# Moving the splits of Wo and the turns of the attention output in the last units of a fused transformer block

## The chip, the cores and the metric

The kernel runs on one core of a Trainium2 chip. The metric is the time of one execution on the device, in microseconds (us). It was run three times; the median is 1302.93 us (1302.89 to 1303.72). The profile comes from one further execution of 1301.86 us.

The engines are named as the profile names them: TensorE (PE; PEld is its weight load), VectorE (DVE), ScalarE (ACT), GpSimd (POOL), and SyncE (SP), which only issues DMA transfers here. Each engine works through its own list of instructions in the order in which the program lists them.

## The reference

For one sequence of S = 2048 tokens with D = 576 values each, the block adds three things: the input, an attention over eight dilated neighbours, and a mixer with an MLP of F = 4608 hidden values.

```python
xn = _layernorm(x)
# attention: 32 heads of 18; token s looks at s, s-2, ..., s-14
qkv = xn @ wqkv
logits = einsum("bhsd,bhswd->bhsw", q, kg) * scale
o = einsum("bhsw,bhswd->bhsd", softmax(logits), vg)
A = o @ wo
# mixer: shift four channel groups by +1, -1, +2, -2 tokens
h = gelu(_layernorm(xn) @ w1)
x1 = xn + shifted(h) @ w2
B = x1 + gelu(_layernorm(x1) @ w3) @ w4
return x + A + B
```

All matmuls work on pairs of a rounded part ("hi") and the rest ("lo") of each operand, and add up the products hi·hi, hi·lo and lo·hi, so that the result has the precision of 32-bit floats.

## The kernel before

The program is one function, `fused_block`. The order of instructions on each engine is the order in which the Python code emits them: nothing is rescheduled. First come the projections to q, k and v, then the mixer, then a long loop that holds the MLP, and at last the output phase.

**The loop over units** (line 759). The MLP is cut into 18 chunks c of 256 hidden values and 4 blocks b of 512 tokens, so 72 units (c, b). A unit has an *up* part and a *down* part:

- `up(c, b, i)`, for i = 0 and 1: 14 matmuls of 128x512 into one accumulator (line 676). ScalarE then makes the gelu twice: hi (line 680) and g32 (line 681, called g in the profile). VectorE makes lo = g32 - hi (line 682).
- `down(*prev, j)`, for j = 0 to 3: the second matmul of the *previous* unit, for token tile j of 128 tokens, 12 matmuls of 128x288 (line 696) into an accumulator `ps`. VectorE then adds it to Y (line 699; "the addition" below). The accumulators come from the pool `psb`, a ring of three: a fourth tile can be begun only when the first of the three has been added.

In the units before the last six, VectorE works on the attention in between, in small steps. The last six units have extra work, written by hand into the loop. They are numbered from the end: z = u - 72, so z = -6 to z = -1. After z = -1 come four more down tiles (line 828), for the unit z = -1 itself, and then the output phase (line 835).

**What is prepared there.** The output phase multiplies the attention output by Wo, tile by tile of 128 tokens (t = 0 to 15), with the transposed attention output standing. Two things have to be ready for it:

- *Wo as hi and lo.* `load_wo(k)` loads a part of Wo into the buffer `rawf` (two buffers): k = 0 and k = 2 are two slices of 128 rows each, k = 4 is the remaining 64 rows, loaded twice. `split_wo(k)` (by way of `split_w`) rounds it on ScalarE (line 167) and subtracts on VectorE (line 168). The three calls are the first, second and last part of Wo.
- *The attention output, transposed, as hi and lo,* in four blocks b of 512 tokens. `load_o(b)` loads a block in token order. `o_turn(b, t)` turns one of its four tiles on VectorE with two transposes of 32x32 squares (lines 129 and 130) into the staging tile ST (`st` in the profile, of which there is one). After the fourth tile, `put` writes ST to DRAM in four transfers (line 137; `xd`), and `get` reads the block back transposed in two (line 142) into a tile that `o_block` provides: `xt` for blocks 0 and 1, the tiles `x1n` of the MLP's input for blocks 2 and 3. `split_x` makes hi and lo of it (lines 148 to 155), half by half.

Before the change these calls stood as follows.

| unit | before the up part | in the up part | between the down tiles | after |
|---|---|---|---|---|
| z = -5 | | | `o_turn(0, j)` | `load_o(2)` |
| z = -4 | `load_wo(0)` | `get` of block 0 | `o_turn(1, j)` | `load_o(3)` |
| z = -3 | `split_wo(0)`, `load_wo(2)` | `get` of block 1 | `split_x` of block 0 | |
| z = -2 | `split_wo(2)`, `load_wo(4)` | `o_turn(2, 0)` to `o_turn(2, 3)` | | `get` of block 2 |
| z = -1 | `split_wo(4)` | `split_x` of block 1 | `o_turn(3, j)` | |
| last four tiles | | | `get` of block 3 behind j = 0; `split_x` of block 2 | |

`split_x` of block 3 stands in the output phase, at t = 4 and 5.

Of the kernel before, what the change touches and what calls it, by code (L numbers as in the profile page):

```python
# [45 lines left out]
def fused_block(ctx, tc, x, wqkv, wo, w1, w2, w3, w4, out):  # L46
# [80 lines left out]
    def turn(src, t):  # L127
        c = slice(32 * t, 32 * t + 32)
        dve.transpose(ST[:, 4:20, c], src[:, :512].rearrange("p (j c) -> p j c", c=32))  # L129
        dve.transpose(ST[:, 0:4, c].rearrange("p (a j) c -> p a j c", a=2),  # L130
                      src[:, 512:].rearrange("p (j c) -> p j c", c=32)[:, None, :, :]
                      .to_broadcast([128, 2, 2, 32]))

    def put(key):
        xd[key] = dram.tile([5, 128, 512], F32, name="xd", bufs=4)
        for q in range(4):
            sp.dma_start(dram_ap(xd[key], 128 * q, [[512, 32], [32 * 512, 20], [1, 128]]),  # L137
                         ST[32 * q:32 * q + 32])

    def get(key, xt):  # L140
        for k in ((0, 3), (3, 5)):
            sp.dma_start(xt[:, 4 + k[0]:4 + k[1], :].bitcast(F32),
                         xd[key][k[0]:k[1]].rearrange("k p c -> p k c"))

    def split_x(xt, part=None):
        raw = xt.bitcast(F32)
        if part != 1:
            act.copy(RT[64:128, :], raw[64:128, 4, :])
            act.copy(xt[0:64, 4, :], raw[0:64, 4, :])
            dve.tensor_tensor(xt[64:128, 4, :], raw[64:128, 4, :], RT[64:128, :].bitcast(F32),  # L150
                              op=ALU.subtract)
        for h in range(2) if part is None else (part,):
            hi, lo = slice(2 * h, 2 * h + 2), slice(2 * h + 5, 2 * h + 7)
            act.copy(xt[:, hi, :], raw[:, lo, :])
            dve.tensor_tensor(xt[:, lo, :], raw[:, lo, :], raw[:, hi, :], op=ALU.subtract)
# [10 lines left out]
    def split_w(dst_hi, dst_lo, raw):  # L166
        act.copy(dst_hi, raw)  # L167
        dve.tensor_tensor(dst_lo, raw, dst_hi.bitcast(F32), op=ALU.subtract)  # L168
# [44 lines left out]
    def ring_block(key):  # L213
        if key not in xring:
            xring[key] = ring.tile([128, 9, 512], F32R, name="xt", tag="xt")
        return xring[key]
# [290 lines left out]
    def split_w3(f):  # L507
        if f >= NF:
            return
        t = W3[f] = wp.tile([128, 10, 128], F32R, name="W3", bufs=3)  # L510
        split_w(t[:, 0:5, :], t[:, 5:10, :], raws[f][:, :640].rearrange("p (k c) -> p k c", k=5))
# [9 lines left out]
    def n_turn(t, zpool):  # L521
        z = zpool.tile([128, D], F32, name="rz", tag="rz")
        act.activation(z, Y[:, t, :], AF.Identity, bias=RS[2][:, t, 0:1], scale=RS[2][:, t, 1:2])
        turn(z, t % 4)
        if t % 4 == 3:
            put(("n", t // 4))
# [130 lines left out]
    def bg(us, late=True):  # L657
        if state["gen"] is None or state["done"]:
            return
        state["debt"] = min(state["debt"] + us, 1.5)  # L660
        while state["debt"] > 0 and (late or not state["hold"]):
            cost = next(state["gen"], False)
            if cost is False:
                state["done"] = True
                return
            state["hold"] = cost is None
            state["debt"] -= cost or 0.0
# [4 lines left out]
    def up(c, b, i):  # L672
        f = c * C + i
        ps = psa.tile([128, 512], F32, name="p1", tag="a")
        for n, (a, w) in enumerate(PAIRS):
            pe.matmul(ps, W3[f][:, w, :], x1n[b][:, a, :], start=n == 0, stop=n == len(PAIRS) - 1)  # L676
        hi = hp.tile([128, 512], F32R, name=f"hi{i}")
        g32 = hp.tile([128, 512], F32, name="g32")
        lo = hp.tile([128, 512], F32R, name=f"lo{i}")
        act.activation(by_token(hi), in_order(ps), AF.Gelu_apprx_tanh)  # L680
        act.activation(by_token(g32), in_order(ps), AF.Gelu_apprx_tanh)  # L681
        dve.tensor_tensor(lo, g32, hi.bitcast(F32), op=ALU.subtract)  # L682
        hid[c, b, i] = (hi, lo)
# [26 lines left out]
    def open_wo():  # L710
        nonlocal wop, opool, Wo
        apc.__exit__(None, None, None)
        wop = tc.tile_pool(name="wop", bufs=1, reuse_waits="tile")
        opool = wop.__enter__()
        Wo = opool.tile([128, 10, D], F32R, name="Wo")
# [3 lines left out]
    def load_wo(k):  # L719
        r = worw[k] = wp.tile([128, 640 + D], F32, name="rawf", bufs=2)  # L720
        if k < 4:
            sp.dma_start(r[:, :2 * D].rearrange("p (k c) -> p k c", k=2),
                         wo[k * 128:(k + 2) * 128, :].rearrange("(k p) c -> p k c", p=128))
        else:
            dup_tail(r[:, :D], wo, 0, D)

    def split_wo(k):
        n = 2 if k < 4 else 1
        split_w(Wo[:, k:k + n, :], Wo[:, 5 + k:5 + k + n, :],
                worw[k][:, :n * D].rearrange("p (k c) -> p k c", k=n))  # L730
# [3 lines left out]
    def load_o(b):  # L734
        if b < NB:
            otile[b] = opool.tile([128, 4, D], F32, name="ot", bufs=2)
            for q in range(4):
                sp.dma_start(otile[b][32 * q:32 * q + 32], quads(od, b, q))

    def load_xa(t):  # L740
        xagain[t] = tp.tile([128, D], F32, name="rz", tag="rz")
        sp.dma_start(xagain[t], xf[t * 128:(t + 1) * 128, :])

    def o_turn(b, t):
        turn(otile[b][:, t, :], t)
        if t == 3:
            put(("o", b))

    def o_block(b):
        if b < 2:  # L750
            xo[b] = ring_block(("o", b))
        else:
            xo[b] = xp.tile([128, 9, 512], F32R, name=f"x1n{b}")
        return xo[b]
# [4 lines left out]
    for u, (c, b) in enumerate(units):  # L759
        if u == 2:  # L760
            ap_pool = apc.__enter__()
            state["gen"] = attention(ap_pool)
            next(state["gen"])
        r = RATE[b] / 6 if u >= 4 else 0.0
        z = u - NU
        if z == -6:
            while not state["done"]:
                bg(1e9)
            open_wo()
            load_o(0)  # L770
            load_o(1)
        if z == -4:
            load_wo(0)
        if z == -3:
            split_wo(0)
            load_wo(2)
        if z == -2:
            split_wo(2)
            load_wo(4)
        if z == -1:  # L780
            split_wo(4)
        for i in range(C):
            bg(r, False)
            up(c, b, i)
            if (u, i) in ((0, 0), (1, 0)):
                get(("n", u + 2), x1n[u + 2])
            for t in LATE.get((u, i), ()):
                n_turn(t, tp)
            if u in (1, 2) and i == 0:
                split_x(x1n[u + 1], 0)  # L790
            if z in (-4, -3) and i == 1:
                get(("o", z + 4), o_block(z + 4))
            if z == -2:
                o_turn(2, 2 * i)
                o_turn(2, 2 * i + 1)
            if z == -1:
                split_x(xo[1], i)
        if b == 3:
            split_w3(2 * c + 3)
        if prev is not None:  # L800
            for j in range(4):
                bg(r, j == 1)
                down(*prev, j)
                if u in (1, 2) and j == 1:
                    split_x(x1n[u + 1], 1)
                if z in (-5, -4, -1):
                    o_turn({-5: 0, -4: 1, -1: 3}[z], j)
                if z == -3 and j > 1:
                    split_x(xo[0], j - 2)
            if z in (-5, -4):  # L810
                load_o(z + 7)
            if z == -2:
                get(("o", 2), o_block(2))
        if b == 1:
            split_w3(2 * c + 2)
        if b == 2:
            split_w4(2 * c + 2)
            load_f(2 * c + 4)
        if b == 0 and c > 0:
            split_w4(2 * c + 1)  # L820
            load_f(2 * c + 3)
        if 4 <= u < 4 + 4 * NT:
            if u % 4 == 0:
                load_xa(u // 4 - 1)
            if u % 4 == 2:
                add_x(u // 4 - 1)
        prev = (c, b)
    for j in range(4):
        down(*prev, j)
        if j == 0:  # L830
            get(("o", 3), o_block(3))
        if j > 1:
            split_x(xo[2], j - 2)
# [51 lines left out]
```

## Time and profile before

| | |
|---|---|
| median of three runs | 1302.93 us (1302.89 to 1303.72) |
| profiled execution | 1301.86 us, its span 1300.1 us |
| TensorE busy | 1287.7 us, 99% |
| TensorE's weight loads | 1186.9 us, 91% |
| VectorE busy | 935.5 us, 72% |
| ScalarE busy | 361.7 us, 28% |
| GpSimd busy | 38.1 us, 3% |
| granted TensorE clock, mean | 0.997 |

The span is the time from the first to the last instruction. A line of a timeline reads: start in us from the span's start, length in us, engine, line of the program, operation, output <- inputs, shape and type, count; several like instructions in a row are one line, and square brackets give the idle time of the engine just before and what ended it. The names are those of the program with buffer numbers left out. "SPq" is the issue of a transfer by SyncE, and its length is that of the issue, not of the transfer. The granted clock is the share of TensorE's full clock that it was given in a stretch.

### The profile page before, as it was taken

What the parts mean: (1) busy time and instruction counts of PE and PEld (TensorE: products, weight loads), DVE (VectorE), ACT (ScalarE), POOL (GpSimd) and SP (SyncE); (2) the same over time, 40 slices, a digit from 0 to 9 for tenths busy, and PEclk for the clock granted to TensorE, in tenths of its full rate; (3) what the DMA queues carried; (4) which work ended last, traced back from release to release, by engine and by line L of the source; (5) the groups of instructions that cost most, each with busy time, mean ns of one, the idle gap of its engine ahead of it and who ended that gap; (6) DMA issues with size and microseconds to landing.
All of it is one profiled execution on the core that took longest, in us unless ns stands there. A gap on an engine that the chain in (4) does not pass through costs nothing.

```text
span 1300.1 us, 18507 instructions
## 1 busy us (share of the span) xinstructions
PE 1287.7 (99%) x7678; PEld 1186.9 (91%) x7678; DVE 935.5 (72%) x1336; ACT 361.7 (28%) x601; POOL 38.1 (3%) x108
## 2 busy tenths in 40 slices
PE   8999999999999999999999999999999999999898
PEld 8999998899899899999989899999999899999798
DVE  6456535778676778888878888878898877946642
ACT  3322226515422222132232232132232232122300
POOL 2011100021000000000000000000000000000000
PEclk9999999999999999999999999999999999999899
DMA  7646874345602120231221222122222102058542
GB/s 211 155 111 145 172 164 145 102 123 138 214 29 72 40 89 20 81 100 33 68 81 40 81 72 90 44 69 64 66 73 81 43 26 81 20 120 208 154 145 83
DMA packets 157828, 125.20 MB, mean 96 GB/s; under 512 B 72608, under 2 KB 129824, under 8 KB 157744
## 3 DMA queue, kind: packets, MB, share of 16 engines
q1 hardware_dynamic: 157744, 124.02, 34.4%
q8 instruction: 60, 0.98, 0.3%
q14 instruction: 24, 0.20, 0.0%
HBM read 83.56 MB, written 39.39 MB: 95 GB/s over the span
## 4 chain that ended last, share of the span: by engine, by line
PE 93%; DMA 3%; DVE 3%; SPq 1%; ACT 0%; issue 0%; POOL 0%; DVEq 0%
PE ps L696 33%; PE p L676 33%; PE ps L182 18%; PE ps L431 4%; PE ps L276 3%; DMA xd<-st 2%; DVE st L129 1%; DMA xt<-xd 1%; PE ps L446 1%; SPq L137 1%; PE ps L104 0%; DVE Y L699 0%; DMA x1n<-xd 0%; DVE bn L86 0%; PE p L853 0%
## 5 line engine op out<-in xcount | busy, mean ns | idle before, releaser
L696 PE MATMUL ps<-W,hi 128*128 128x288 f32 x2304 | 399.8, 295 | 5.2 <-DVE Y L699 5.2
L696 PEld LDWEIGHTS ps<-W,hi 128*128 128x128 f32 x2304 | 340.3, 188 | 12.1 <-DVE Y L699 5.7
L680 ACT ACTIVATE hi<-p 128x512 fp32r<-128x512 f32 x144 | 86.2, 598 | 576.1 <-PE p L676 576.1
L696 PE MATMUL ps<-W,lo 128*128 128x288 f32 x1152 | 245.8, 295 | 0.0
L676 PE MATMUL p<-x1n,W 128*128 128x512 f32 x1008 | 236.0, 391 | 0.0
L676 PE MATMUL p<-xt,W 128*128 128x512 f32 x1008 | 234.5, 389 | 0.0
L676 PEld LDWEIGHTS p<-x1n,W 128*128 128x128 f32 x1008 | 188.4, 189 | 37.2
L699 DVE TENSOR_TENSOR Y<-ps,Y 128x576 f32<-128x576 f32 x288 | 212.1, 749 | 13.5 <-PE ps L696 13.5
L676 PEld LDWEIGHTS p<-xt,W 128*128 128x128 f32 x1008 | 187.3, 188 | 36.9
L682 DVE TENSOR_TENSOR lo<-g,hi 128x512 fp32r<-128x512 f32 x144 | 99.4, 691 | 158.1 <-ACT g L681 158.0
L696 PEld LDWEIGHTS ps<-W,lo 128*128 128x128 f32 x1152 | 185.9, 188 | 0.0
L182 PE MATMUL ps<-WQ,xt 128*128 128x432 f32 x672 | 134.4, 359 | 0.0
L182 PEld LDWEIGHTS ps<-WQ,xt 128*128 128x128 f32 x672 | 125.5, 188 | 5.4
L628 DVE TENSOR_TENSOR prod<-q,k 128x1152 f32<-128x1152 f32 x64 | 86.4, 1350 | 0.0
L631 DVE TENSOR_REDUCE L<-prod 128x64 f32<-128x1152 f32 x64 | 86.2, 1347 | 0.0
L681 ACT ACTIVATE g<-p 128x512 f32<-128x512 f32 x144 | 85.3, 592 | 0.0
L612 DVE TENSOR_TENSOR o<-o,prod 128x1152 f32<-128x1152 f32 x56 | 75.6, 1350 | 0.0
L608 DVE TENSOR_TENSOR prod<-v,L 128x1152 f32<-128x1152 f32 x56 | 75.6, 1350 | 0.0
L167 ACT CAST W<-rawf 128x640 fp32r<-128x640 f32 x72 | 50.3, 700 | 70.5 <-PE ps L696 69.2
L168 DVE TENSOR_TENSOR W<-rawf,W 128x640 fp32r<-128x640 f32 x72 | 56.3, 785 | 0.0
L182 PE MATMUL ps<-W,h 128*128 128x288 f32 x384 | 53.5, 295 | 0.0
L182 PEld LDWEIGHTS ps<-W,h 128*128 128x128 f32 x384 | 51.9, 188 | 0.1
(108 smaller groups left out, 888.2 us busy)
## 6 DMA issues: line engine op xcount, KB each, us to landing
xd<-st SPq DMA_DIRECT2D x48, 320.0 KB, 6.0
qkvd<-stg SPq DMA_DIRECT2D x24, 432.0 KB, 3.5
rawf<-in_B_w_dram SPq DMA_DIRECT2D x36, 288.0 KB, 3.1
rawf<-in_B_w_dram SPq DMA_DIRECT2D x36, 256.0 KB, 2.9
xt<-xd SPq DMA_DIRECT2D x8, 768.0 KB, 5.1
xin<-in_A_x_dram SPq DMA_DIRECT2D x16, 288.0 KB, 3.8
q<-qkvd SPq DMA_DIRECT2D x8, 576.0 KB, 3.9
k<-qkvd SPq DMA_DIRECT2D x8, 576.0 KB, 5.6
```

The lines of the kernel that those rows point to most:

```text
L168: dve.tensor_tensor(dst_lo, raw, dst_hi.bitcast(F32), op=ALU.subtract)
L182: pe.matmul(ps[:, h, :n], xs(a), ws(b, h), start=i == 0, stop=i == len(PAIRS) - 1)
L608: dve.tensor_tensor(dst, vv, Lf[:, :, w:w + 1].to_broadcast([128, TPP * GH, HD]), op=ALU.mult)
L612: dve.tensor_tensor(o, o, dst, op=ALU.add)
L628: dve.tensor_tensor(prod.rearrange("p (j h) d -> p j (h d)", h=GH), q, k[:, r0:r0 + TPP, :], op=ALU.mult)
L631: dve.tensor_reduce(Lf[:, :, w], prod, axis=AX.X, op=ALU.add)
L676: pe.matmul(ps, W3[f][:, w, :], x1n[b][:, a, :], start=n == 0, stop=n == len(PAIRS) - 1)
L680: act.activation(by_token(hi), in_order(ps), AF.Gelu_apprx_tanh)
L681: act.activation(by_token(g32), in_order(ps), AF.Gelu_apprx_tanh)
L682: dve.tensor_tensor(lo, g32, hi.bitcast(F32), op=ALU.subtract)
L696: pe.matmul(ps[:, k, :HF], h[:, col], w[:, p, k * HF:(k + 1) * HF], start=n == 0, stop=n == len(seq) - 1)
L699: dve.tensor_tensor(yv, ps[:, :, :HF], yv, op=ALU.add)
```

## The change

Five calls are moved. No call is added or dropped.

- `split_wo(2)` goes from the start of z = -2 to the start of z = -1.
- `split_wo(4)` goes from the start of z = -1 to behind the first of the last four down tiles.
- The four turns of block 2 go from the up part of z = -2 (two behind each `up`) to between the down tiles of z = -2 (one behind each).
- The four turns of block 3 stay between the down tiles of z = -1, but two stand behind each of the last two tiles, not one behind each of the four.
- `get` of block 2 goes from the end of z = -2 to the second half of the up part of z = -1.

```diff
         if z == -2:
-            split_wo(2)
             load_wo(4)
         if z == -1:
-            split_wo(4)
+            split_wo(2)
...
-            if z == -2:
-                o_turn(2, 2 * i)
-                o_turn(2, 2 * i + 1)
+            if z == -1 and i == 1:
+                get(("o", 2), o_block(2))
...
-                if z in (-5, -4, -1):
-                    o_turn({-5: 0, -4: 1, -1: 3}[z], j)
+                if z in (-5, -4, -2):
+                    o_turn({-5: 0, -4: 1, -2: 2}[z], j)
+                if z == -1 and j > 1:
+                    o_turn(3, 2 * j - 4)
+                    o_turn(3, 2 * j - 3)
...
-            if z == -2:
-                get(("o", 2), o_block(2))
...
     for j in range(4):
         down(*prev, j)
         if j == 0:
+            split_wo(4)
             get(("o", 3), o_block(3))
```

In the lists of instructions below, a line is line of the program, operation, output <- inputs, and the shape of the output; numbers behind names tell buffers apart.

On VectorE, in unit z = -2 as it was: behind the last subtraction for block 0 (line 155) of z = -3 come the second part of Wo, then lo of the first `up`, then the first turns of block 2.

```order
 L168 TENSOR_TENSOR Wo<-rawf,Wo 128x1152
-L682 TENSOR_TENSOR lo_10945<-g_10944,hi_10943 128x512
-L129 STREAM_TRANSPOSE st<-ot 128x16x32
-L130 STREAM_TRANSPOSE st<-ot 128x4x32
-L129 STREAM_TRANSPOSE st<-ot 128x16x32
-L130 STREAM_TRANSPOSE st<-ot 128x4x32
-L682 TENSOR_TENSOR lo_10970<-g_10969,hi_10968 128x512
```

Two more turns follow, and only then the four additions (line 699). With the change the same place has both lo and the first addition ahead of the first turn, and each further addition ahead of a turn:

```order
 L155 TENSOR_TENSOR xt<-xt 128x1024
+L682 TENSOR_TENSOR lo_10943<-g_10942,hi_10941 128x512
+L682 TENSOR_TENSOR lo_10964<-g_10963,hi_10962 128x512
+L699 TENSOR_TENSOR Y<-ps,Y 128x576
+L129 STREAM_TRANSPOSE st<-ot 128x16x32
+L130 STREAM_TRANSPOSE st<-ot 128x4x32
+L699 TENSOR_TENSOR Y<-ps,Y 128x576
```

The subtraction for Wo's second part has moved behind the fourth turn.

On ScalarE, in the same unit: the cast of Wo's second part (128x1152) stood ahead of the four gelus, and now stands behind them.

```order
 L154 CAST xt<-xt 128x1024 x2
+L680 ACTIVATE hi_10941<-p_10926 128x512
+L681 ACTIVATE g_10942<-p_10926 128x512
+L680 ACTIVATE hi_10962<-p_10947 128x512
+L681 ACTIVATE g_10963<-p_10947 128x512
 L167 CAST Wo<-rawf 128x1152
-L680 ACTIVATE hi_10943<-p_10928 128x512
-L681 ACTIVATE g_10944<-p_10928 128x512
```

On VectorE, in unit z = -1 and the last four down tiles, with the change: behind the additions of the tiles j = 0 to 2 stand two turns of block 3, then the addition of j = 3 and two more turns; the first of the last four additions follows, and behind it the last part of Wo (128x576).

```order
+L129 STREAM_TRANSPOSE st<-ot 128x16x32
+L130 STREAM_TRANSPOSE st<-ot 128x4x32
+L699 TENSOR_TENSOR Y<-ps,Y 128x576
+L168 TENSOR_TENSOR Wo<-rawf,Wo 128x576
+L699 TENSOR_TENSOR Y<-ps,Y 128x576 x2
+L150 TENSOR_TENSOR x1n_11086<-x1n_11086,rt 64x512
+L155 TENSOR_TENSOR x1n_11086<-x1n_11086 128x1024
+L699 TENSOR_TENSOR Y<-ps,Y 128x576
```

The piece begins with the last of these turns. Before, each turn stood behind one addition, and the last part of Wo ahead of the unit.

On SyncE the order of the transfers is the same before and after, since the moved `get` still stands between the two `put` of blocks 2 and 3. On GpSimd nothing moves.

## The prediction

> **What bounds the kernel.** I read three views in this order: the chain that ended last, the list of what TensorE waited for, and the timeline of TensorE around its longest wait. The first two:
>
> ```profile
> PE 93%; DMA 3%; DVE 3%; SPq 1%; ACT 0%; issue 0%; POOL 0%; DVEq 0%
> ...
> PE ps L696 <- DVE Y L699: 5.2, 2, 4.6
> ```
>
> TensorE sets the time, so work on another engine counts only where TensorE waits for it. In the large matmul phases it waited twice, 5.2 us in all, and one wait is 4.6 of it. The timeline shows that one in unit z = -2:
>
> ```profile
> 1198.11 6.52 PE L676 MATMUL p<-x1n,W 128*128 128x512 f32 x28
> 1204.47 0.69 PE L696 MATMUL ps<-W,hi 128*128 128x288 f32 x4
> ...
> 1213.97 1.33 PE L696 MATMUL ps<-W,hi 128*128 128x288 f32 x4 [4.58 <-DVE Y L699]
> ...
> 1217.01 7.88 PE L676 MATMUL p<-x1n,W 128*128 128x512 f32 x28
> 1224.73 0.69 PE L696 MATMUL ps<-W,hi 128*128 128x288 f32 x4
> ```
>
> After the gap the same 28 up matmuls take 7.88 us, not 6.52, and four down matmuls 1.33, not 0.69. The table of stretches gives the granted clock in the column after POOL (first number of a row: length; then the busy time of each engine):
>
> ```profile
> 1185.41:1198.11 12.70, 12.70 (x78) 11.60 (x77) 9.56 (x16) 6.33 (x10) 0.00 (x0) 1.00 1.06 299
> ...
> 1213.97:1217.01 3.04, 3.04 (x12) 3.04 (x13) 1.27 (x2) 0.00 (x0) 0.00 (x0) 0.50 0.87 167
> 1217.01:1224.73 7.72, 7.72 (x30) 6.25 (x29) 2.80 (x4) 2.93 (x5) 0.00 (x0) 0.81 0.64 157
> ```
>
> An undisturbed unit lasts 12.70 us at clock 1.00. From the down tiles of z = -2 to those of z = -1 the profile has 1224.73 - 1204.47 = 20.26 us, so **7.56 us are lost here**. They divide thus: the up part takes 1204.47 - 1198.11 = 6.36, so four down tiles take 6.34 and one 1.585; the fourth was due at 1204.47 + 3 x 1.585 = 1209.23 and began at 1213.97, 4.74 late. What remains, 1.59 + 6.36 = 7.95, took 10.76: 2.81 lost to the lower clock.
>
> Why was it late? A down tile's accumulator comes from a ring of three, so the fourth needs VectorE to have added the first into Y:
>
> ```profile
> 1198.80 0.39 SPq L722 DMA_DIRECT2D rawf<-in_A_wo_dram  x1
> ...
> 1206.34 1.16 ACT L167 CAST Wo<-rawf 128x1152 fp32r<-128x1152 f32 x1 [8.59 <-DMA rawf<-in_A_wo_dram]
> ...
> 1207.53 1.36 DVE L168 TENSOR_TENSOR Wo<-rawf,Wo 128x1152 fp32r<-128x1152 f32 x1 [6.27 <-ACT Wo L167]
> 1208.81 0.68 DVE L682 TENSOR_TENSOR lo<-g,hi 128x512 fp32r<-128x512 f32 x1
> ...
> 1209.41 0.70 DVE L129 STREAM_TRANSPOSE st<-ot 128x512 f32<-128x512 f32 x1
> ...
> 1211.02 0.65 DVE L682 TENSOR_TENSOR lo<-g,hi 128x512 fp32r<-128x512 f32 x1
> ...
> 1213.19 2.05 DVE L699 TENSOR_TENSOR Y<-ps,Y 128x576 f32<-128x576 f32 x3
> ```
>
> Wo's second part lands 7.5 us after its issue. Its cast stands ahead of the unit's gelus on ScalarE, its subtraction ahead of everything of the unit on VectorE, and four turns ahead of the additions. VectorE idles 6.27 us, then does 5.66 us of work (1207.53 to 1213.19) before the first addition.
>
> **The change, unit z = -2.** No instruction is added or removed; SyncE's issues keep their order. The cast and the subtraction go behind the unit, the turns between its additions. The nearest rows are unit z = -4, where nothing stands ahead of the first addition, z = -3 for the pace of TensorE, and z = -5 for turns between additions:
>
> ```profile
> 1170.53 0.72 DVE L699 TENSOR_TENSOR Y<-ps,Y 128x576 f32<-128x576 f32 x1
> ...
> 1171.98 0.72 DVE L699 TENSOR_TENSOR Y<-ps,Y 128x576 f32<-128x576 f32 x1
> ...
> 1172.71 6.52 PE L676 MATMUL p<-xt,W 128*128 128x512 f32 x28
> ...
> 1177.21 0.69 DVE L682 TENSOR_TENSOR lo<-g,hi 128x512 fp32r<-128x512 f32 x1 [2.26 <-ACT g L681]
> ...
> 1179.07 0.69 PE L696 MATMUL ps<-W,hi 128*128 128x288 f32 x4
> ...
> 1181.00 0.75 DVE L699 TENSOR_TENSOR Y<-ps,Y 128x576 f32<-128x576 f32 x1
> ...
> 1196.72 0.76 DVE L699 TENSOR_TENSOR Y<-ps,Y 128x576 f32<-128x576 f32 x1 [0.18 <-PE ps L696]
> ```
>
> The first addition comes 1.93 after the first down matmul: here at 1206.40. Its accumulator is free 0.65 later (an addition with its turn repeats every 1.45, from 1170.53 to 1171.98; two turns take 1.61, from 1209.41 to 1211.02, so the addition is 0.65), at 1207.05, 2.2 ahead of 1209.23. **The wait goes, and so its clock loss: 7.56 us.** Each further addition waits for TensorE, whose 1.585 per tile is longer than 1.45. The addition that waited for the third tile began 4.95 after the unit's down start (1191.77 by the 12.70 period), 0.20 behind the tile's end; so the fourth begins at 1204.47 + 6.34 + 0.20 = 1211.01 and the last turn ends at 1212.46. The write of the third block begins there, 0.8 before the 1213.29 below. On ScalarE the cast of Wo (1.16) starts when its data lands, at 1206.34, now that the unit's gelus no longer queue behind it. On VectorE the subtraction of 1.28 (1207.53 to 1208.81) follows the last turn and is over at 1213.74. The up part of z = -1 starts at 1210.81, and its first line 682 can come only 4.50 later (1172.71 to 1177.21), at 1215.31: this idle stretch hides both. More than 7.56 can't be won here, since TensorE's only other wait of this kind is one of 0.60 at 331.46 us (its row stands below).
>
> **Unit z = -1 and the last four down tiles.** Down tiles of z = -1 start at 1204.47 + 12.70 = 1217.17, the last four at 1223.51, the output phase at 1229.85. From line 682 to the first addition VectorE's order is as before, where that addition came 3.44 after the down start and no gap followed:
>
> ```profile
> 1217.92 0.75 DVE L168 TENSOR_TENSOR Wo<-rawf,Wo 128x576 fp32r<-128x576 f32 x1
> ...
> 1228.17 0.75 DVE L699 TENSOR_TENSOR Y<-ps,Y 128x576 f32<-128x576 f32 x1
> ...
> 1229.48 0.69 PE L696 MATMUL ps<-W,hi 128*128 128x288 f32 x4
> ```
>
> So it comes at 1220.61 and frees its accumulator 0.65 ahead of the fourth tile (1221.93), as in the profile. The second follows at 1221.28, the third at 1217.17 + 4.95 = 1222.12, over at 1222.79. Now two turns of the fourth block stand here, and the first waits until the staging tile st, the only one, has been written out. What that write takes is seen twice, from its first issue to the issue that reads it back:
>
> ```profile
> 1189.02 6.67 SPq L137 DMA_DIRECT2D xd<-st  x4
> ...
> 1199.79 0.91 SPq L142 DMA_DIRECT2D xt<-xd  x2
> ...
> 1213.29 4.17 SPq L137 DMA_DIRECT2D xd<-st  x4
> 1221.94 0.91 SPq L142 DMA_DIRECT2D x1n<-xd  x2
> ```
>
> 8.65 us alone, 10.77 beside other transfers. I take 8.65, since here as there Wo's loads are over: ready at 1221.1, before the turn. At 10.77 it is 1223.3, 0.5 late. The two turns take 1.61, which puts the fourth addition at 1224.40 to 1225.05, two more turns to 1226.66, the first of the last four additions to 1227.3, Wo's last subtraction (0.67) to 1228.0, the second addition to 1228.65. TensorE needs these buffers at 1226.68 (fourth addition), 1228.27 and 1229.85: slack 1.6, 0.96 and 1.2. Queued behind a waiting turn on VectorE are these additions, and TensorE waits for them; both bounds of the write cost nothing, because 0.5 is less than 0.96. Beyond that cover each further microsecond is lost whole. Wo's last part, whose split moves from the start of z = -1 to here, is whole at 1228.0, before the output phase reads it; its cast (0.67, ahead of it on ScalarE) lies beside VectorE's turns.
>
> The fourth block's write starts at 1226.66, 3.2 ahead of the output phase; before, it was 3.3:
>
> ```profile
> 1234.11 4.16 SPq L137 DMA_DIRECT2D xd<-st  x4
> ...
> 1237.42 7.82 PE L182 MATMUL ps<-Wo,xt 128*128 128x288 f32 x58
> ...
> 1247.84 0.62 ACT L148 CAST rt<-x1n 64x512 fp32r<-64x512 f32 x1 [17.66 <-DMA x1n<-xd]
> ...
> 1253.21 0.69 DVE L150 TENSOR_TENSOR x1n<-x1n,rt 64x512 fp32r<-64x512 f32 x1
> ```
>
> VectorE came to that block 4.7 after its first cast (1247.84 + 0.62), which hides 0.1. The third block is read only from output tile 8 on. So nothing is given back, and the sum is -7.56.
>
> [...] A shorter rest of the wait may or may not bring the clock down. The trace has one short wait:
>
> ```profile
> 331.46 0.80 PE L696 MATMUL ps<-W,hi 128*128 128x288 f32 x4 [0.60 <-DVE Y L699]
> ...
> 331.46:335.00 3.54, 3.54 (x21) 3.23 (x22) 3.54 (x5) 0.00 (x0) 0.00 (x0) 1.00 0.64 127
> ```
>
> 0.60 us left the clock at 1.00; 4.58 us brought 0.50. [...] By the longer row it would cost 2.81 more; no row between the two decides.
>
> **The rivals.** *A rest of the wait stays.* The chain that ended last comes to the unit's first line 682 by a transfer:
>
> ```profile
> 1200.21 8.60 DMA xt<-xd
> 1208.82 0.68 DVE lo L682
> ```
>
> If that were a true wait, line 682 would still start at 1208.82, the unit's other one at 1209.4, the first addition at 1210.0, and its buffer would be free at 1210.7, 1.5 after 1209.23. The gain is then 6.1, or 3.3 with the clock loss: 1296.8 or 1299.7. Against it: line 682 reads only hi and g, which ScalarE wrote, and VectorE was busy with Wo up to that moment (1207.53 and 1.28).
>
> *It ends slower.* The one staging tile holds up the fourth block's turns in z = -1. With a write of 17.3 us, twice 8.65, the turn starts at 1229.8, 7.0 late; less 0.96 and with the 2.81 of the clock that is 8.85 lost against 7.56 won: 1304.2. It decides from a write of 16.0 us on (10.33 from its start to 1222.79, the slack of 0.96, and an idle time of 7.56 - 2.81 = 4.75). The longest seen is 10.77.
>
> *The change doesn't do what it says.* The wait for Wo's second part moves along into z = -1 and stalls TensorE there as much: 1302.9. The load would have to land some 6 us later than 1206.34, though nothing ahead of it on SyncE has moved.
>
> **How the numbers follow.** The profiled execution took 1301.86 us, 1.76 around its span of 1300.1; less 7.56 it is 1294.30. The median of the three runs, 1302.93, lies 1.07 above it; by that the changed kernel has **1295.4**. Chances: forecast 0.88, a rest of the wait 0.06, slower 0.03, no effect 0.03. The runs before spread from the profile's 1301.86 to 1303.72, which puts the forecast alone at 1294.3 to 1296.2; the rest of 1.5 us ends at 1296.8. Range 1294.2 to 1297.0. About 0.2%, 2.6 us, is what a measurement here can tell from no change: faster 0.94, same 0.03, slower 0.03.
>
> **What would show it.** Right: no wait of TensorE for line 699 but the 0.60; the down starts 12.70 apart through z = -1, clock 1.00 from 1204 on; the output phase from 1229.85; the turns of the fourth block start without a wait for st. Wrong: a gap at the fourth down tile of z = -2 (a rest), a gap in the last four tiles with VectorE idle at line 129 (staging), or ScalarE idle for Wo in z = -1 beyond 1210 (the load).

## The result and the profile after

| | before | after |
|---|---|---|
| median | 1302.91 us (1302.86 to 1303.72, 4 executions) | 1295.07 us (1294.01 to 1295.98, 4 executions) |
| profiled execution, its span | 1301.86 us, 1300.1 us | 1294.73 us, 1292.9 us |
| mean granted clock of it | 0.997 | 1.000 |

The ratio is 0.9938, with a 95% interval of 0.9921 to 0.9955: 0.6% faster. Beside the later experiments the changed kernel ran five more times: 1294.06 us (1293.88 to 1294.36), ratio 0.9944 (0.9932 to 0.9957) to the kernel before, which there had a median of 1301.34 us.

The view to read first is again the list of what TensorE waited for (engine, line, what it waited for: us in total, times, longest). This is its row for the additions:

```profile
PE ps L696 <- DVE Y L699: 0.4, 1, 0.4
```

Of 5.2 us there is 0.4 left, and that is the short wait at 331.72 us, which was there before with 0.60. The timeline of TensorE in the last units, up parts (line 676), first down matmuls and the start of the output phase:

```profile
1198.55 6.52 PE L676 MATMUL p<-x1n,W 128*128 128x512 f32 x28
1204.90 0.69 PE L696 MATMUL ps<-W,hi 128*128 128x288 f32 x4
...
1209.66 0.69 PE L696 MATMUL ps<-W,hi 128*128 128x288 f32 x4
...
1211.24 6.52 PE L676 MATMUL p<-x1n,W 128*128 128x512 f32 x28
1217.60 0.69 PE L696 MATMUL ps<-W,hi 128*128 128x288 f32 x4
...
1230.29 14.96 PE L182 MATMUL ps<-Wo,xt 128*128 128x288 f32 x112
```

The down tiles of z = -2 and z = -1 start 12.70 apart, and the output phase 12.69 after that. The fourth tile starts at 1209.66, 4.76 after the first, with no bracket: nothing was waited for. Its clock, by the table of stretches (the column after POOL):

```profile
1198.55:1211.24 12.69, 12.69 (x78) 11.59 (x77) 8.81 (x15) 3.33 (x5) 0.00 (x0) 1.00 0.96 268
1211.24:1223.94 12.70, 12.70 (x78) 11.60 (x77) 10.15 (x15) 5.76 (x9) 0.00 (x0) 1.00 0.59 110
1223.94:1230.29 6.35, 6.35 (x50) 6.35 (x49) 6.32 (x13) 3.13 (x4) 0.00 (x0) 1.00 0.83 255
```

TensorE is busy in every one of the 31.74 us, at full clock. Why, the timeline of ScalarE and VectorE in z = -2 shows:

```profile
1203.05 0.69 DVE L682 TENSOR_TENSOR lo<-g,hi 128x512 fp32r<-128x512 f32 x1 [1.35 <-ACT g L681]
...
1206.76 1.16 ACT L167 CAST Wo<-rawf 128x1152 fp32r<-128x1152 f32 x1 [0.57 <-DMA rawf<-in_A_wo_dram]
1206.83 0.75 DVE L699 TENSOR_TENSOR Y<-ps,Y 128x576 f32<-128x576 f32 x1
...
1212.94 1.32 DVE L168 TENSOR_TENSOR Wo<-rawf,Wo 128x1152 fp32r<-128x1152 f32 x1
```

Wo's data lands as late as before (1206.76), but only its own cast waits for it, and for 0.57 us instead of 8.59. The first addition starts at 1206.83, not 1213.19.

The span fell by 7.2, not 7.56, since in this execution TensorE reached z = -2 0.44 later (1198.55 against 1198.11). That difference comes from before the place of the change.

### The profile page after: what moved, and what is told of

Read it like the earlier page. It is cut to its first block, busy times and chain, and to the rows that moved or that the text cites. A ratio compares the mean times of both kernels' runs of the same rounds, so it can differ in the third digit from the quotient of the medians.

```text
span 1292.9 us, 18505 instructions
## 1 busy us (share of the span) xinstructions
PE 1285.0 (99%) x7678; PEld 1184.8 (92%) x7678; DVE 935.6 (72%) x1336; ACT 362.0 (28%) x601; POOL 38.1 (3%) x108
## 4 chain that ended last, share of the span: by engine, by line
PE 94%; DMA 2%; DVE 2%; ACT 1%; SPq 0%; issue 0%; ACTq 0%
PE ps L696 35%; PE p L676 34%; PE ps L182 17%; PE ps L431 4%; PE ps L276 3%; DMA xd<-st 1%; PE ps L446 1%; PE ps L104 1%; DMA xt<-xd 0%; DMA raw<-in_A_wqkv_dram 0%; DMA x1n<-xd 0%; DVE st L129 0%; SPq L137 0%; PE p L853 0%; ACT rz L523 0%
```

## The experiments

All are judged by the time, by TensorE's waits and by the granted clock. They ran in two groups of four, each group beside the kernel before on one chip; the ratio is to those executions.

**1. Wo alone.** From the kernel before, only the split of Wo's second part moves. The split of the last part stays at the start of z = -1, and the turns stay in the up part.

```diff
         if z == -2:
-            split_wo(2)
             load_wo(4)
         if z == -1:
+            split_wo(2)
             split_wo(4)
```

> From the kernel before, Wo's second part alone is moved: its split stands ahead of z = -1 (with the last part behind it); all turns stay where they were. Theory (the wait for Wo's transfer made the whole loss; the four turns ahead of the additions fit in): by the rows of the changed kernel the first line 682 of z = -2 starts at 1203.05, two turns end at 1205.3, the other line 682 runs from 1206.2 to 1206.8, two turns end at 1208.4 and the first addition at 1209.1, 0.6 ahead of the fourth down tile (1209.66): no gap, clock 1.00, time as the changed kernel, 1295.1 (1294.0 to 1296.2). Rival (the 3.2 us of turns ahead of the additions are a cause of their own): a gap of 1 us or more at the fourth down tile of z = -2, 1296 to 1300.

Measured: 1294.8 us (1293.71 to 1295.38), ratio 0.9949 (0.9937 to 0.9961). The only wait for an addition is one of 0.5 near 331 us. The four turns ahead of the additions end in time on VectorE:

```profile
1207.56 0.27 DVE L130 STREAM_TRANSPOSE st<-ot 128x128 f32<-128x128 f32 x1
1207.75 2.18 DVE L699 TENSOR_TENSOR Y<-ps,Y 128x576 f32<-128x576 f32 x3
```

The first addition starts at 1207.75, and the up part of the unit at 1197.86, so the fourth tile is due at 1197.86 + 6.36 + 4.76 = 1208.98. Its accumulator is free 0.65 later, at 1208.40, which leaves 0.6, as expected. Moving the split of Wo's second part is enough by itself, and the other moves add nothing to it that can be measured. They only widen the slack: in the profile after it is 1209.66 - (1206.83 + 0.65) = 2.2.

One of the five executions, of 1295.14 us, has a mean clock of 0.999, which was not expected; the profiled one has 1.000. The mean also takes in the end of the span behind the last matmul, 3.3 us in the profile after, of which the last 0.97 had a clock of 0.50 and cost nothing. By an estimate from the span, about 1.3 us of that kind would make a 0.999. Whether TensorE lost time in that execution is not known, since it has no trace.

**2. Wo put back.** From the changed kernel, the opposite: only the split of the second part goes back.

```diff
         if z == -2:
+            split_wo(2)
             load_wo(4)
-        if z == -1:
-            split_wo(2)
```

> From the changed kernel, the split of Wo's second part alone is put back ahead of z = -2; the turns stay moved. Theory: its data lands at 1206.8, the gelus run from 1207.8 on, both lines 682 end at 1210.5, the first addition at 1211.15, 1.5 after 1209.66: a gap of 1.4 to 1.5 at the fourth down tile. If the clock falls only after a longer idle time: 1296.6 and matmuls of unchanged length; if any gap of this size costs the 2.81 us of the lower clock too: 1299.4. Rival (turns were the cause): no gap, 1295.1.

Measured: 1296.53 us (1295.62 to 1299.2), ratio 0.9969 (0.9959 to 0.9980). TensorE in the profiled execution, and its clock:

```profile
1212.26 0.80 PE L696 MATMUL ps<-W,hi 128*128 128x288 f32 x4 [1.88 <-DVE Y L699]
...
1214.21 7.89 PE L676 MATMUL p<-x1n,W 128*128 128x512 f32 x28
...
1212.26:1213.15 0.89, 0.89 (x6) 0.89 (x7) 0.89 (x3) 0.00 (x0) 0.00 (x0) 1.00 0.00 0
1213.15:1214.21 1.06, 1.06 (x9) 1.06 (x8) 1.06 (x3) 0.00 (x0) 0.00 (x0) 0.72 0.05 15
1214.21:1217.00 2.79, 2.79 (x8) 2.23 (x8) 2.79 (x7) 0.00 (x0) 0.00 (x0) 0.50 0.00 0
1217.00:1218.00 1.00, 1.00 (x5) 0.83 (x5) 0.36 (x2) 0.00 (x0) 0.00 (x0) 0.98 0.00 0
```

The gap is there, 1.88 instead of 1.5. ScalarE's cast shows why it is longer:

```profile
1207.70 1.16 ACT L167 CAST Wo<-rawf 128x1152 fp32r<-128x1152 f32 x1 [9.04 <-DMA rawf<-in_A_wo_dram]
```

Wo landed 0.9 later than the 1206.8 assumed, in a unit whose first down matmul was only 0.56 later (1205.46 against 1204.90). The surprise is the clock: it was 1.00 when TensorE went on, and fell to 0.50 about 1.4 us later (0.89 + 1.06 - 0.59, the last being the part of the 0.72 row at the low clock). It did not do so in each execution: four of the seven have a mean clock of 1.000 and 1295.6 to 1296.5 us, three have 0.999 and 1297.7 to 1299.2 us. Both of the expected times occur. TensorE waited for additions twice more in the profiled execution, 1.6 us together (3.5 less 1.88), and its mean clock of 0.999 is what the one low stretch, 3.41 us long (1213.62 to 1217.03), makes by itself: 1.7 us lost in a span of 1297.3.

**3. Two turns more.** As 2, with two turns ahead of the second line 682.

```diff
+            if z == -2 and i == 0:
+                o_turn(2, 0)
+                o_turn(2, 1)
...
-                if z in (-5, -4, -2):
+                if z in (-5, -4) or z == -2 and j > 1:
```

> As the run before this, and two of the four turns of block 2 ahead of the other line 682 of z = -2, as they stood before the change: 1.61 us more ahead of the first addition. Theory: the gap is 3.0 to 3.1. Without the lower clock 1298.2, with 2.81 of it 1301.0. Together with the runs with 1.5 and 4.58 this shows between which idle times the clock falls. Rival (ScalarE's late gelus set the additions, turns fill idle time): the gap stays 1.5, 1296.6.

Measured: 1299.17 us (1297.21 to 1302.94, 12 executions), ratio 0.9988 (0.9980 to 0.9997).

```profile
1213.23 1.33 PE L696 MATMUL ps<-W,hi 128*128 128x288 f32 x4 [3.71 <-DVE Y L699]
```

The gap is 3.71, where 3.0 to 3.1 was expected, and 1.83 longer than in run 2. Two turns are 1.61, and the cast started 0.33 later as well (2.57 behind the unit's first down matmul, against 2.24 in run 2). So behind a late Wo the turns do cost, though in run 1, without it, four of them cost nothing. The executions fall into three groups: two at clock 1.000 (1297.2 and 1298.2 us), five at 0.999 (1298.5 to 1299.2), five at 0.997 (1301.0 to 1302.9).

**4. One turn per tile.** From the changed kernel, the turns of block 3 stand one behind each tile of z = -1.

```diff
-                if z in (-5, -4, -2):
-                    o_turn({-5: 0, -4: 1, -2: 2}[z], j)
-                if z == -1 and j > 1:
-                    o_turn(3, 2 * j - 4)
-                    o_turn(3, 2 * j - 3)
+                if z in (-5, -4, -2, -1):
+                    o_turn({-5: 0, -4: 1, -2: 2, -1: 3}[z], j)
```

> From the changed kernel, the four turns of block 3 stand one behind each down tile of z = -1 again. Theory: the first turn is reached at 1221.7 and st is free at 1221.8, so VectorE waits about 0.1, then each addition with its turn takes 1.45, less than TensorE's 1.585; the first of the last four additions ends at 1227.6 against 1228.7: no gap, time as the changed kernel, 1295.1 (1294.0 to 1296.2); putting two turns behind each of the last two tiles is worth nothing. Rival (the earlier turn waits for the staging tile and holds the additions): VectorE idle at line 129 of over 0.5 and a gap in the last four tiles, 1296 or more.

Measured: 1294.16 us (1294.1 to 1295.07), ratio 0.9947 (0.9934 to 0.9960); no gap in the last units, and no idle time of VectorE at the first turn, whose row has no bracket:

```profile
1221.09 0.70 DVE L129 STREAM_TRANSPOSE st<-ot 128x512 f32<-128x512 f32 x1
```

Delaying these turns is worth nothing.

**5. The changed kernel again,** beside runs 6 to 8.

> The changed kernel once more, beside the runs that follow, on one chip with them. Theory (two terms: the wait of 4.7 us is gone in every execution, the loss by the lower clock of up to 2.8 us in those that had it): where the executions of the kernel before spread from 1300.1 to 1303.7 with mean clocks 0.999 and 0.997, this one shows 1.000 in all of them and 1294 to 1296. Rival (the clock falls by itself, whatever TensorE waits for): some executions with 0.999 or less and 1296.5 or more.

Measured: 1294.06 us (1293.88 to 1294.36), mean clock 1.000 in all five. Of the 15 executions of the kernel before beside it, 4 have 0.999 and 11 have 0.997, at 1300.5 to 1303.3 us; of the 19 beside runs 1 to 4, 11 and 8, at 1300.1 to 1303.1 us. So all 34 executions of the kernel before have a mean clock below 1.000, the nine of the changed kernel have 1.000, and the mean of the kernel before varied from one execution to the next. The rival falls with that, but for the one 0.999 in run 1, which stays open.

**6. Four turns at once.** From the changed kernel, all turns of block 3 stand behind the first tile of z = -1.

```diff
-                if z == -1 and j > 1:
-                    o_turn(3, 2 * j - 4)
-                    o_turn(3, 2 * j - 3)
+                if z == -1 and j == 0:
+                    for t in range(4):
+                        o_turn(3, t)
```

> From the changed kernel, all four turns of block 3 stand behind the first down tile of z = -1. Theory (the cover of the additions is used up by VectorE's order alone): st is free at 1221.8, the turns end at 1225.0, the second addition at 1225.7, and the first of the last four tiles, due at 1223.94, waits 1.75: 1296.9 in executions whose clock stays, up to 1299.7 in those where it falls (it fell behind 1.88 us of idle time in one profile). Rival (TensorE is covered here by the ring of accumulators): no gap, 1295.1.

Measured: 1296.45 us (1295.97 to 1297.31), ratio 0.9963 (0.9950 to 0.9975).

```profile
1225.75 0.77 PE L696 MATMUL ps<-W,hi 128*128 128x288 f32 x4 [1.67 <-DVE Y L699]
```

A gap of 1.67 where 1.75 was expected, at the first of the last four tiles. The clock stayed at 1.000 in all five executions. The cover in z = -1 is thus as thin as the prediction had it.

**7. The write twice.** From the changed kernel, `put` of block 2 issues its four transfers a second time, the same data to the same place.

```diff
-        for q in range(4):
+        for q in list(range(4)) * (2 if key == ("o", 2) else 1):
             sp.dma_start(dram_ap(xd[key], 128 * q,
```

> From the changed kernel, the write of the third block to DRAM is issued twice, so that the staging tile is held about twice as long (same data to the same place). Theory (the slower rival of the prediction, with its price): the write takes about 16 us instead of 8.65, the fourth block's first turn starts at about 1229.2, 6.0 later; less the slack of 0.96 TensorE idles about 5.0 in the last four tiles; 1300.1 with the clock kept, 1302.9 with all of the 2.81. Rival (the staging tile is not what holds the turns): at most 1 us of gap, 1295.1 to 1296.

Measured: 1298.14 to 1301.16 us in ten executions, whose median is 1300.1; an eleventh took 7313.92 us, for a reason that is not known, and is left out. The ratio is 0.9990 (0.9980 to 0.9999). SyncE, VectorE and TensorE:

```profile
1212.43 10.71 SPq L137 DMA_DIRECT2D xd<-st  x8
1227.33 0.91 SPq L142 DMA_DIRECT2D x1n<-xd  x2
...
1227.66 0.71 DVE L129 STREAM_TRANSPOSE st<-ot 128x512 f32<-128x512 f32 x1 [4.96 <-DMA xd<-st]
...
1230.05 0.80 PE L696 MATMUL ps<-W,hi 128*128 128x288 f32 x4 [3.38 <-DVE Y L699]
```

The chain is the one expected: the turn waits for the staging tile, the additions behind it, TensorE behind them. The write took 14.9 us (1212.43 to 1227.33), not 16, so the gap is 3.38, not 5.0; the lower clock adds to it, since nine of the ten executions have a mean of 0.999 or less. That the median is the very 1300.1 expected with the clock kept is chance: the gap was shorter, and the clock was not kept.

**8. The cast alone.** From the changed kernel, only the cast goes back ahead of the gelus of z = -2; the subtraction stays ahead of z = -1. `split_wo` gets two arguments for this, and its cast and subtraction are lines 732 and 734 there.

```diff
         if z == -2:
+            split_wo(2, subtract=False)
             load_wo(4)
         if z == -1:
-            split_wo(2)
+            split_wo(2, cast=False)
```

> From the changed kernel, only the cast of Wo's second part (ScalarE) goes back ahead of the gelus of z = -2; its subtraction (VectorE) stays ahead of z = -1. Theory (the unit's gelus behind the waiting cast set the first addition; the subtraction of 1.28 lies in the time in which VectorE waits for them anyway): the second g ends as late as in the run with both put back, a gap of 1.4 to 1.9 at the fourth down tile of z = -2, 1296.5. Rival (VectorE's queue sets it): the gap is shorter by about 1.3, 1295.1 to 1295.5.

Measured: 1296.65 us (1296.17 to 1298.64), ratio 0.9968 (0.9955 to 0.9980), as run 2. ScalarE, VectorE and TensorE:

```profile
1206.93 1.16 ACT L732 CAST Wo<-rawf 128x1152 fp32r<-128x1152 f32 x1 [8.36 <-DMA rawf<-in_A_wo_dram]
...
1209.10 0.69 DVE L682 TENSOR_TENSOR lo<-g,hi 128x512 fp32r<-128x512 f32 x1 [7.13 <-ACT g L681]
...
1209.43 0.61 ACT L681 ACTIVATE g<-p 128x512 f32<-128x512 f32 x1
...
1210.07 0.69 DVE L682 TENSOR_TENSOR lo<-g,hi 128x512 fp32r<-128x512 f32 x1 [0.28 <-ACT g L681]
...
1211.49 0.80 PE L696 MATMUL ps<-W,hi 128*128 128x288 f32 x4 [1.40 <-DVE Y L699]
```

VectorE has no Wo ahead of it, yet waits for the late gelus. So a first part of the old gap comes from ScalarE's queue: a cast that waits for a transfer, with four gelus behind it that could have run (in the profile after they are over by 1206.2, ahead of the cast). The gap is 0.48 shorter than in run 2, and that is not the subtraction: the cast started 1.75 behind the unit's first down matmul (1205.18), in run 2 2.24. In the kernel before it started 1.87 behind (1206.34 - 1204.47), so by run 8 about 1.5 of its 4.58 are ScalarE's, an estimate. The other 3.1 are close to the 3.2 of the four turns behind it on VectorE (run 3 has half of them). Two of the five executions have a mean clock of 0.999 (1298.0 and 1298.6 us), three 1.000.

## Why the prediction was right

1295.4 was forecast, 1295.07 measured. That the two are so close is in part luck: the 7.56 come from one profile, the 1.07 added to it from three other executions, and beside runs 5 to 8 the medians lie 7.28 apart (1301.34 and 1294.06). The mechanism does not hang on it. Its steps against the profile after, whose last units lie 0.43 later (1204.90 against 1204.47):

| step | forecast | profile after, less 0.43 |
|---|---|---|
| first addition of z = -2 | 1206.40 | 1206.40 |
| end of the turns of block 2, start of the Wo subtraction | 1212.46 | 1212.51 |
| write of block 2, issue to reading back | 8.65 | 8.65 |
| first turn of block 3 | 1222.79 | 1222.80 |
| output phase | 1229.85 | 1229.86 |

These rows carry the third and fourth line; the third is 1221.69 - 1213.04:

```profile
1213.04 4.17 SPq L137 DMA_DIRECT2D xd<-st  x4
1221.69 0.91 SPq L142 DMA_DIRECT2D x1n<-xd  x2
...
1223.23 0.70 DVE L129 STREAM_TRANSPOSE st<-ot 128x512 f32<-128x512 f32 x1
```

*The wait* (4.74): right in place and size; runs 1, 2 and 8 show the cause, and divide it more sharply than the prediction did, which named the cast, the subtraction and the turns together. The cast held the gelus, the subtraction cost nothing, and the turns cost only behind the late gelus: without the cast there, run 1 has no gap.

*The clock* (2.81): right for the profiled execution, but not a constant. The kernel before had a mean clock of 0.999 in 15 of 34 executions, with a median of 1300.77 us, and of 0.997 in the other 19, with one of 1301.57. A sum made against one profile carries this with it.

*A rest of the wait.* The chain had led into line 682 by the transfer of block 1. In the profile after, line 682 starts at 1203.05, while that transfer, issued at 1200.12, takes 8.6 or more: it was never waited for. The other half of that rival, what a wait of 1.5 would cost, was open between two prices; runs 2 and 8 have times near each, in different executions. That a wait of 1.5 costs its length alone, as the first price has it, no run shows for every execution: in the traces 1.40 us (run 8) and 1.67 (run 6) left the clock at 1.00, and behind 1.88 (run 2) it was at 0.50.

*It ends slower.* The mechanism is real (run 7), and its price fits: a write of 14.9, short of the 16.0 from which it was to decide, ended just below the kernel before. A write of 16.0 was not tried. The size assumed for a doubled write, 17.3, was too long.

*No effect:* fell with the first profile.

## What to carry to other kernels

An instruction that waits for a transfer should stand behind all work of its engine that is ready and wanted, not at the start of the loop body in which its data arrives: here one cast of 1.16 us waited 8.59 us and held four gelus, and with them TensorE. When several edits are made together, undo and keep each one alone: here one of five moved calls, `split_wo(2)`, brought everything, and the others nothing that could be measured. And a stall of TensorE can be dearer than its length, by an amount that differs from execution to execution: with the 1.88 us of run 2, four of seven executions have a mean clock of 1.000 and 1295.6 to 1296.5 us, three 0.999 and 1297.7 to 1299.2. So the kernel with the stall also scattered more, over 3.6 us against 2.0 of the changed kernel (1294.01 to 1295.98).

## What the runs showed of the hardware

These rows show the clock around the longest wait in two kernels (length, TensorE's busy time first, the clock after POOL). Run 2, whose wait of 1.88 us ended at 1212.26:

```profile
1210.38:1212.26 1.88, 0.00 (x1) 0.00 (x1) 1.88 (x4) 0.43 (x1) 0.00 (x0) 1.00 0.58 111
...
1213.62:1217.03 3.41, 3.41 (x11) 2.85 (x10) 3.41 (x8) 0.00 (x0) 0.00 (x0) 0.50 0.00 0
1217.04:1220.45 3.41, 3.41 (x16) 2.78 (x16) 0.70 (x3) 1.48 (x3) 0.00 (x0) 1.00 0.58 113
```

The kernel before, whose wait of 4.58 us ended at 1213.97:

```profile
1209.39:1213.06 3.67, 0.00 (x0) 0.00 (x0) 3.67 (x10) 0.74 (x2) 0.00 (x0) 1.00 0.09 24
1213.07:1219.89 6.82, 5.92 (x19) 5.34 (x20) 3.59 (x7) 0.00 (x0) 0.00 (x0) 0.50 0.79 161
1219.89:1224.73 4.84, 4.84 (x23) 3.95 (x22) 1.38 (x2) 2.93 (x5) 0.00 (x0) 1.00 0.46 129
```

In run 2 the clock was at 0.50 for 3.41 us, from 1.36 behind the end of the wait on. In the kernel before it was at 0.50 for 6.82 us, of which 0.90 (6.82 - 5.92) lie in the idle time and cost nothing. By these rows the 3.41 us cost TensorE 1.7, an estimate, and the 5.92 about 3.0, against 2.81 by the sum of the prediction.

The wait for an addition in the last units, the clock behind it in the one execution that has a trace, and the executions of the kernel with a mean clock below 1.000:

| | wait, us | clock in the stretch behind it | mean below 1.000 |
|---|---|---|---|
| kernel before | 4.58 | 0.50 (1213.97 to 1217.01) | 34 of 34 |
| run 3 | 3.71 | 0.50 (1213.23 to 1216.27) | 10 of 12 |
| run 7 | 3.38 | 0.79 (1230.05 to 1232.00), then 0.50 (to 1234.00) | 9 of 10 |
| run 2 | 1.88 | 0.72 (1213.15 to 1214.21), then 0.50 (to 1217.00) | 3 of 7 |
| run 6 | 1.67 | 1.00 (1225.75 to 1232.00) | 0 of 5 |
| run 8 | 1.40 | 1.00 (1211.49 to 1218.00) | 2 of 5 |

With the three longer waits 53 of 56 executions have a mean below 1.000, with the three shorter ones 5 of 17. Why the executions of one kernel differ is not shown, since only one of each has a trace. Whether it is the idle time that brings the clock down, or something else that goes with it, was not tried.
